# Block 0's x in half rows, W_in in two later parts, block 1's diagonal products in four slots

## The chip, the core and the metric

One kernel, launched once on one NeuronCore of a Trainium2 chip. The metric is device time in microseconds (us), the median of nine runs. TensorE is called PE here, VectorE DVE, ScalarE ACT, GpSimd POOL and SyncE SP, as the profile names them.

## What is computed

The reference is a causal depthwise convolution with seven softmaxed taps for each of eight heads, followed by a two-layer network with an exact GELU:

```
w   = softmax(weight, axis=-1)                       # [8 heads, 7 taps]
xp  = x with 6 zero rows ahead of each sequence      # x: [8, 4096, 192] float32
a[b,s,h,g] = sum_k w[h,k] * xp[b, s+k, h, g]         # 24 channels a head
h   = a.reshape(32768, 192) @ w_in                   # w_in: [192, 2048]
out = (0.5*h*(1+erf(h/sqrt(2)))) @ w_out             # w_out: [2048, 192], float32 out
```

## The kernel before, in words

The 32768 tokens are two halves of 16384, which lie on partitions 0 to 63 and 64 to 127. Each half is cut into 35 blocks: six of 256 tokens (`WS`), then 29 of 512. The 192 channels stand on 64 partitions as three planes (`p`, `NP = 3`), channel 3i+p in plane p. All engine programs are written out by hand; semaphores are the only order between them.

A block goes through these steps. SP loads x in four quarters (`load`, L329). DVE transposes 32x32 tiles into `xT` (`trans`, L526), one instruction a plane. From block 2 on, DVE makes the convolution with seven multiply-adds a plane (`conv`, L552 and L559) and writes `xc` in bf16. PE multiplies `xc` with W_in (`mm1`, L760) in slices into one of two PSUM buffers `hp`; ACT applies the GELU to each slice (L681) and writes `gT`; PE multiplies `gT` of the block before with W_out (`mm2`, L791, `mm2_t` from block 6 on, L824). A slice of `mm1` may start only when the GELU two slices back is done (`S_GELU`). The results leave through `osb`.

Blocks 0 and 1 (`PC`) are different, because DVE would be too slow for a start: their convolution is made on PE (`pconv`, L711), as products of 64x64 diagonal matrices `dg`, one for each tap, with a bf16 copy `xTb` of `xT`. Their four accumulations (`kinds`: plane 0, plane 1, and two halves of plane 2) are called kd 0 to 3; `conv_out` (L191 on ACT, L193 on DVE) copies them from PSUM to `xc`. Block 0's fourteen products for kd 0 and 1 and for kd 2 and 3 come ahead of everything; block 1's stand behind slices 4 and 5 of block 0's `mm1` (the dictionary `behind`, L729).

The start, engine by engine, in program order:

- **SP**: the taps `wsb` (L872), two quarters of block 0's x; then a wait on the first part of W_in (`S_WIN[0]`, L874); block 1's x, W_out in four parts (L878), block 2's and block 3's x. ACT issues the other two quarters of block 0's x. In block 0 a partition holds eight consecutive tokens, and one run of 1440 numbers (5760 bytes) is read for it, both channel halves with it, of which 96 numbers a token are used.
- **POOL**: W_in's first part (256 of 1024 columns a half, L384, two DMAs that cast to bf16), the identity mask (L393), the second part (256 columns) and the third (512); then the halo columns, block 1's bf16 casts (L213, on `xT` of block 1), and the bf16 casts of W_out (L457), which the first `mm2` waits for.
- **DVE**: memsets, the softmax of the taps (L467 to L485), `dg` (L491), block 0's three transposes, two `conv_out` pieces, copies of W_in's parts to the other half's partitions (`dup`, L502; slices 4 to 7 of block 0's `mm1` need them, `S_DUPE`), block 1's transposes, the last `dup`, block 1's six `conv_out` pieces, and then block 2.
- **ACT**: the exponentials, block 0's three bf16 casts (L630), four `conv_out` pieces, then GELUs.
- **PE**: sixteen products of zeros (L695), block 0's diagonal products, then slices.

Of the kernel before, what the change touches and what calls it, by code (L numbers as in the profile page):

```python
# [11 lines left out]
def bass_lightweight_conv__then__act_gelu_exact_kernel(  # L12
# [7 lines left out]
    B, SEQ, D = x.shape  # L20
    H, KS = weight.shape
    D2, F = moe_w_in.shape
# [6 lines left out]
    TB = 512  # L29
# [19 lines left out]
    HX = 8  # L49
# [53 lines left out]
    def sem(name):  # L103
        return es.enter_context(nc.semaphore(name))

    def ap(t, off, pat):
        return bass.AP(t, off, pat)

    with es:
# [23 lines left out]
        ob = pst("ob", [128, 2048])  # L133

        S_WSB = sem("S_WSB")
        S_WIN = [sem("S_WIN%d" % i) for i in range(3)]
        S_WOUT = [sem("S_WOUT%d" % i) for i in range(4)]
        S_WOG = sem("S_WOG")
        S_XIN = [sem("S_XIN%d" % i) for i in range(NX)]
# [6 lines left out]
        S_DG = sem("S_DG")  # L146
        S_HOT = sem("S_HOT")
        S_CAST = [sem("S_CAST%d" % i) for i in range(len(PC))]
        S_PC = sem("S_PC")
        S_PCE = sem("S_PCE")  # L150
        S_PCA = sem("S_PCA")
# [52 lines left out]
        NCV = NP * KS  # L204
        FQ = F // 8
        FH = F // 2
        FP = [0, FQ, 2 * FQ, FH]

        WG = [0, 4, 2, 6]

# [105 lines left out]
        def load(e, n, qs=(0, 2, 1, 3), sm=None):  # L316
            mb = WS[n] // 32
            if n >= NX:
                e.wait_ge(S_TR, NP * (n - NX + 1))
            for q in qs:  # L320
                off = ((q // 2) * HALF + OFF[n]) * D + DQ * (q % 2)
                if n == 0:

                    dst = [[TB // 32 * DQ, 32], [1, mb * D - DQ]]
                    src = [[mb * D, 32], [1, mb * D - DQ]]
                else:
                    dst = [[TB // 32 * DQ, 32], [DQ, mb], [1, DQ]]
# [52 lines left out]
        @block.gpsimd  # L380
        def _(g):
            def win_in(c0, c1, sm):
                for hf in range(2):
                    g.dma_start(  # L384
                        ap(win, 64 * hf * NP * F + c0, [[NP * F, 64], [F, NP], [1, c1 - c0]]),
                        ap(wint, hf * FH + c0, [[NP * F, 64], [F, NP], [1, c1 - c0]]),
                    ).then_inc(sm, 16)

            win_in(FP[0], FP[1], S_WIN[0])
            g.wait_ge(S_MSET, 1)  # L390
            for hf in range(2):
                m = idb[64 * hf : 64 * hf + 64, :]
                g.affine_select(  # L393
                    out=m,
                    in_=m,
                    compare_op=ALU.is_equal,
                    fill=0.0,
                    base=0,
                    pattern=[[-1, 64]],
                    channel_multiplier=1,  # L400
                ).then_inc(S_IDN)
            for i in range(1, 3):
                win_in(FP[i], FP[i + 1], S_WIN[i])

            def halo(n):
                if n == 0:

                    t = xTb[0]
                    g.memset(
                        ap(t, 0, [[NP * XB, 128], [XB, NP], [32, HB]]), 0.0  # L410
                    ).then_inc(S_HALO)
                    for p in range(NP):
                        g.wait_ge(S_TR, p + 1)
                        g.tensor_copy(
                            ap(t, p * XB + 1, [[NP * XB, 128], [32, HB], [1, 31]]),
                            ap(
                                xT[0],
                                p * XW + HX + WS[0] - HL,
                                [[NP * XW, 128], [32, HB], [1, 31]],
                            ),  # L420
                        ).then_inc(S_HALO)
# [25 lines left out]
                g.tensor_copy(dst, src).then_inc(S_HALO)  # L447

            g.wait_ge(S_IDN, 2)
            halo(0)  # L450
            halo(1)
            for p in range(NP):
                cast(g, 1, p)
            for i in range(4):
                g.wait_ge(S_WOUT[i], 16)
                o = 2 * WG[i] * C
                g.tensor_copy(wout[:, o : o + 4 * C], woutf[:, o : o + 4 * C]).then_inc(S_WOG)  # L457
            for n in range(2, NB):
                halo(n)

        @block.vector
        def _(v):
# [34 lines left out]

            def dup(s):

                v.wait_ge(S_WIN[s], 32)  # L500
                for hf in range(2):
                    v.tensor_copy(  # L502
                        ap(
                            win,
                            64 * (1 - hf) * NP * F + FH + FP[s],
                            [[NP * F, 64], [F, NP], [1, FP[s + 1] - FP[s]]],
                        ),
                        ap(
                            win,
                            64 * hf * NP * F + FP[s],  # L510
                            [[NP * F, 64], [F, NP], [1, FP[s + 1] - FP[s]]],
                        ),
                    ).then_inc(S_DUPE)

            def trans(n, p):
                w = WS[n]
                if p == 0:
                    if xin_at(n) > 0:
                        v.wait_ge(S_XIN[n % NX], xin_at(n))
                    if n >= 2 and n - 2 in PC:  # L520
                        wait_pc(v, n - 2, NP - 1)
                    elif n >= 2:
                        v.wait_ge(S_CV, cvd(n - 2))
                    if n >= 1:
                        v.wait_ge(S_HALO, HC[n])
                v.transpose(  # L526
                    ap(xT[n % 2], p * XW + HX, [[NP * XW, 128], [1, w]]),
                    ap(
                        xin[n % NX],
                        p,  # L530
                        [[TB // 32 * DQ, 128], [D if n == 0 else DQ, w // 32], [NP, 32]],
                    ),
                ).then_inc(S_TR)

# [44 lines left out]

            for p in range(NP):  # L580
                trans(0, p)
            conv_out(v, 0, 1)
            conv_out(v, 0, 4)
            dup(0)
            dup(1)
            for p in range(NP):
                trans(1, p)
            dup(2)
            for j in range(len(PIECES)):
                conv_out(v, 1, j)  # L590

# [18 lines left out]
        def _(a):  # L610
# [14 lines left out]
                out=hot[:, 1:2], in_=nc.const_aps.tensor(0.0, (1, 1), F32), func=AF.Gelu  # L625
            ).then_inc(S_HOT)
            a.wait_ge(S_PRO, 9)
            for p in range(NP):
                a.wait_ge(S_TR, p + 1)  # L629
                a.activation(  # L630
                    out=ap(xTb[0], p * XB + HL, [[NP * XB, 128], [1, WS[0]]]),
                    in_=ap(xT[0], p * XW + HX, [[NP * XW, 128], [1, WS[0]]]),
                    func=AF.Copy,
                ).then_inc(S_CAST[0])
# [56 lines left out]
        @block.tensor  # L691
        def _(t):
            t.wait_ge(S_WARM, 1)
            for i in range(16):
                t.matmul(hp[1][:, 0:512], warm[:, 0:128], warm[:, :])  # L695

            def pconv(n, kd, k):

                p, ex, c0, w = kinds(n)[kd]
                if k == KS - 1:  # L700
                    t.wait_ge(S_CAST[PC[n]], p + 1)
                    if n == 0:
                        t.wait_ge(S_DG, 1)
                if k == KS - 2:
# [21 lines left out]
            for kd in order:  # L726
                pconv(*seq[kd].pop(0))

            behind = {  # L729
                (0, 4): [(1, kd, k) for k in taps for kd in (0, 1)],  # L730
                (0, 5): [(1, kd, k) for k in taps for kd in (2, 3)],
            }

            def mm1(n, i):
# [4 lines left out]
                if i == 0:  # L739
                    if n in PC:  # L740
                        wait_pc(t, n, NP - 2)
                    else:
                        t.wait_ge(S_CV, cvd(n))
                if n == 0 and i < 3:
                    t.wait_ge(S_WIN[i], 32)
                if n == 0 and 4 <= i < 7:
                    t.wait_ge(S_DUPE, 2 * (i - 4) + 2)
                for cc in range(c):
                    for p in range(NP):
# [170 lines left out]
```

## Time and profile before

| | |
|---|---|
| median of nine runs | 684.06 us (683.55 to 684.52) |
| the profiled execution | 684.13 us, its span 682.4 us |
| PE busy | 675.5 us, 99% of the span |
| DVE, ACT, POOL busy | 560.9, 536.8, 38.8 us |
| first diagonal product / first slice of `mm1` / first GELU | 7.04 / 8.92 / 10.12 us |
| block 2's first transpose / first slice of block 2's `mm1` | 20.39 / 29.92 us |

All times inside the execution count from the start of the span; 1.7 us of the run's time lie outside it. A line such as `5.96 0.53 DVE xT L526` gives start, length, engine, tile and line of the kernel. "Idle before" is how long the engine stood still, with what released it.

### The profile page before, as it was taken

The page shows a single profiled execution, that of the slowest core. Times are in us where ns is not written, and L with a number is a line of the kernel's source. Part 1 is how long each engine was busy: PE and PEld are TensorE (multiplying, and loading weights), DVE is VectorE, ACT ScalarE, POOL GpSimd, SP SyncE. Part 2 cuts the span into 40 slices and gives each one's busy share as a digit, 9 for nine tenths or more (in the row PEclk, how much of TensorE's full clock was granted, in tenths as well). Part 3 has the DMA queues.
Part 4 walks back from the last instruction along what each step waited for, and adds up shares of the span by engine and source line. Part 5 has one row for each costly group of instructions (what it writes and reads, how often), then busy time and mean ns, then how long its engine had stood idle before and what let it go on. Part 6 is the DMA issues. An engine that isn't in the chain of part 4 may idle for free.

```text
span 682.4 us, 27317 instructions
## 1 busy us (share of the span) xinstructions
PE 675.5 (99%) x12576; PEld 410.2 (60%) x12576; DVE 560.9 (82%) x904; ACT 536.8 (79%) x550; POOL 38.8 (6%) x57
## 2 busy tenths in 40 slices
PE   8999999999999999999999999999999999999998
PEld 4899755555555555555555555555555555555556
DVE  6899979888889888898888898888898888988611
ACT  6799988877777877777877788777778777778772
POOL 5025100000000000000000000000000000000000
PEclk9999999999999999999999999999999999999999
DMA  9345322234342244332244422334322444310123
GB/s 227 72 110 129 84 60 66 45 81 95 96 93 52 46 96 94 95 73 52 67 94 95 94 65 47 81 94 96 93 51 47 95 94 96 79 45 21 48 49 94
DMA packets 132994, 54.79 MB, mean 80 GB/s; under 512 B 126480, under 2 KB 132752, under 8 KB 132880
## 3 DMA queue, kind: packets, MB, share of 16 engines
q1 hardware_dynamic: 130960, 51.50, 32.2%
q8 instruction: 98, 1.61, 1.0%
q0 software_dynamic: 1248, 0.79, 0.9%
q10 hardware_dynamic: 672, 0.76, 0.4%
q14 instruction: 16, 0.13, 0.1%
HBM read 28.66 MB, written 25.17 MB: 79 GB/s over the span
## 4 chain that ended last, share of the span: by engine, by line
PE 96%; ACT 2%; DMA 1%; issue 1%; DVE 0%; SPq 0%; ACTq 0%
PE hp L760 47%; PE ob L824 43%; PE ob L791 5%; ACT gT L681 2%; DMA xin<-in_x_dram 1%; PE ob L711 0%; ACT xc L191 0%; ACT osb L269 0%; DVE osb L311 0%; DVE xT L526 0%; ACT xTb L630 0%; SPq L872 0%; DVE osb L280 0%; SPq L329 0%; ACTq L629 0%
## 5 line engine op out<-in xcount | busy, mean ns | idle before, releaser
L681 ACT ACTIVATE gT<-hp 128x1024 bf16<-128x1024 f32 x512 | 522.8, 1023 | 130.0 <-PE hp L760 126.7
L760 PE MATMUL hp<-xc,win 64*64 64x512 bf16 (+2 forms) x6048 | 419.2, 366 | 2.2 <-issue 0.8
L824 PE MATMUL ob<-gT,wout 64*64 64x512 bf16 x5376 | 366.3, 376 | 0.0
L559 DVE SCALAR_TENSOR_TENSOR acc<-xT,wcol,acc 128x512 f32<-128x512 f32 (+1 forms) x495 | 314.5, 702 | 0.0
L760 PEld LDWEIGHTS hp<-xc,win 64*64 64x64 bf16 (+1 forms) x6048 | 189.9, 106 | 135.4 <-ACT gT L681 2.5
L824 PEld LDWEIGHTS ob<-gT,wout 64*64 64x64 bf16 x5376 | 172.1, 118 | 123.0
L311 DVE STREAM_TRANSPOSE osb<-ob 128x512 f32<-128x512 f32 x84 | 74.3, 887 | 101.0 <-PE ob L824 101.0
L526 DVE STREAM_TRANSPOSE xT<-xin 128x512 f32<-128x512 f32 (+1 forms) x105 | 78.6, 798 | 4.5 <-DMA xin<-in_x_dram 4.5
L559 DVE SCALAR_TENSOR_TENSOR xc<-xT,wcol,acc 128x512 bf16<-128x512 f32 (+1 forms) x99 | 65.2, 715 | 0.0
L447 POOL COPY xT<-xT 128x18 f32<-128x18 f32 x30 | 27.9, 928 | 505.0 <-DVE xT L526 482.6
L791 PE MATMUL ob<-wout,gT 64*128 64x192 bf16 x1024 | 52.9, 243 | 0.3
L791 PEld LDWEIGHTS ob<-wout,gT 64*128 64x128 bf16 x1024 | 44.9, 94 | 5.2 <-PE ob L791 0.6
L552 DVE TENSOR_SCALAR acc<-xT,wcol 128x512 f32<-128x512 f32 (+1 forms) x90 | 37.6, 474 | 1.1
L282 ACT ACTIVATE osb<-ob 128x192 f32<-128x192 f32 x4 | 1.3, 330 | 9.5 <-PE ob L791 9.5
L280 DVE COPY osb<-ob 128x192 f32<-128x192 f32 x4 | 1.4, 358 | 8.4 <-PE ob L791 8.4
L695 PE MATMUL hp<-warm 128*128 128x512 bf16 x16 | 5.5, 517 | 1.3 <-DVE warm L463 1.3
L269 ACT ACTIVATE osb<-ob 128x384 f32<-128x384 f32 x12 | 5.8, 486 | 0.0
L654 ACT ACTIVATE acc<-xT,wcol 128x256 f32<-128x256 f32 (+1 forms) x9 | 5.2, 575 | 0.0
L695 PEld LDWEIGHTS hp<-warm 128*128 128x128 bf16 x16 | 1.9, 126 | 4.3 <-issue 2.5
L384 POOL DMA_DIRECT2D win<-in_moe_w_in_dram x6 | 3.9, 658 | 0.8 <-POOLq L905 0.8
L193 DVE CAST xc<-ob 64x256 bf16<-64x256 f32 (+3 forms) x8 | 2.8, 357 | 1.3 <-PE ob L711 1.1
L502 DVE COPY win<-win 64x768 bf16<-64x768 bf16 (+1 forms) x6 | 3.6, 607 | 0.2
(31 smaller groups left out, 22.1 us busy)
## 6 DMA issues: line engine op xcount, KB each, us to landing
out_dram<-osb SPq DMA_DIRECT2D x122, 192.0 KB, 3.1
xin<-in_x_dram SPq DMA_DIRECT2D x116, 192.0 KB, 4.1
xin<-in_x_dram SPq DMA_DIRECT2D x20, 96.0 KB, 3.7
woutf<-in_moe_w_out_dram SPq DMA_DIRECT2D x4, 384.0 KB, 5.9
win<-in_moe_w_in_dram POOLq DMA_DIRECT2D x4, 96.0 KB, 4.2
win<-in_moe_w_in_dram POOLq DMA_DIRECT2D x2, 192.0 KB, 5.2
out_dram<-osb SPq DMA_DIRECT2D x8, 48.0 KB, 1.9
out_dram<-osb ACTq DMA_DIRECT2D x4, 96.0 KB, 1.9
```

Of the source, the lines that this page charges most:

```text
L269: e.activation(out=dst, in_=src, func=AF.Copy).then_inc(S_EVA)
L311: v.transpose(ap(osb[m % 2], j, [[8 * C, 128], [C // 2, TB // 32], [NP, 32]]), bank(ring(m, j)),).then_inc(S_EV)
L447: g.tensor_copy(dst, src).then_inc(S_HALO)
L526: v.transpose(ap(xT[n % 2], p * XW + HX, [[NP * XW, 128], [1, w]]), ap(xin[n % NX], p, [[TB // 32 * DQ, 128], [D if n == 0 else DQ, w // 3 ...
L552: ins = v.tensor_scalar(a, src, wk, None, ALU.mult)
L559: ins = v.scalar_tensor_tensor(dst, src, wk, a, op0=ALU.mult, op1=ALU.add)
L654: a.activation(out=acc[n % 2][:, p * TB : p * TB + w], in_=ap(xT[n % 2], p * XW + HX, [[NP * XW, 128], [1, w]]), func=AF.Copy, scale=wcol[ ...
L681: a.activation(out=ap(gT[n % 2], i * c * 2 * w, dst), in_=ap(hp[u % 2], 0, src), func=AF.Gelu,).then_inc(S_GELU)
L695: t.matmul(hp[1][:, 0:512], warm[:, 0:128], warm[:, :])
L760: ins = t.matmul(hp[u % 2][fo : fo + fw, o : o + w], ap(win, f1, [[NP * F, 64], [2, fw]]), xc[n % 2][r, p * TB : p * TB + w], start=(p == ...
L791: ins = t.matmul(bank(bb[sub], w=C), gT[m % 2][r, c0 : c0 + 128], wout[r, CH[sub][i] * C : (CH[sub][i] + 1) * C], start=(ph == 0 and i == ...
L824: ins = t.matmul(bank(ring(m, j), slice(64 * h, 64 * h + 64), w), ap(wout, 64 * hf * NF * C + CH[h][i] * C + j, [[NF * C, 64], [NP, 64]],) ...
```

## The change

Block 0's x is read in half rows: 96 numbers (384 bytes) a token, eight runs a partition, so that the four loads move 96 KB each instead of 180 KB. W_in comes in two parts of 512 columns a half instead of three, and POOL issues them all behind the mask and behind a wait for the first result of the softmax, the taps' maximum (`S_PRO` at 1). So `S_WIN[0]`, on which SP waits ahead of block 1's x, now stands for half of W_in. The copies `dup` are four of 256 columns instead of two of 256 and one of 512; the last two stay behind block 1's transposes. Block 0's third bf16 cast goes from ACT to DVE, behind the transposes. Twelve products of zeros instead of sixteen. Block 1's diagonal products stand behind slices 4 to 7 instead of 4 and 5: sixteen and twelve for kd 0 and 1, then sixteen and twelve for kd 2 and 3.

```diff
-        FP = [0, FQ, 2 * FQ, FH]
+        FP = [0, FH // 2, FH]
@@ load
                 if n == 0:
-                    dst = [[TB // 32 * DQ, 32], [1, mb * D - DQ]]
-                    src = [[mb * D, 32], [1, mb * D - DQ]]
+                    src = [[mb * D, 32], [D, mb], [1, DQ]]
@@ POOL
-            win_in(FP[0], FP[1], S_WIN[0])
             g.wait_ge(S_MSET, 1)
...
-            for i in range(1, 3):
+            g.wait_ge(S_PRO, 1)
+            for i in range(2):
                 win_in(FP[i], FP[i + 1], S_WIN[i])
@@ DVE: dup(s) waits for S_WIN[s // 2] and copies FQ columns
             for p in range(NP):
                 trans(0, p)
+            v.wait_ge(S_TR, NP)
+            v.tensor_copy(
+                ap(xTb[0], (NP - 1) * XB + HL, [[NP * XB, 128], [1, WS[0]]]),
+                ap(xT[0], (NP - 1) * XW + HX, [[NP * XW, 128], [1, WS[0]]]),
+            ).then_inc(S_CASTV)
             conv_out(v, 0, 1)
             conv_out(v, 0, 4)
             dup(0)
...
             dup(2)
+            dup(3)
@@ ACT
-            for p in range(NP):
+            for p in range(NP - 1):
                 a.wait_ge(S_TR, p + 1)
@@ PE
-            for i in range(16):
+            for i in range(12):
                 t.matmul(hp[1][:, 0:512], warm[:, 0:128], warm[:, :])
...
             behind = {
-                (0, 4): [(1, kd, k) for k in taps for kd in (0, 1)],
-                (0, 5): [(1, kd, k) for k in taps for kd in (2, 3)],
+                (0, 4): [(1, kd, k) for k in taps[:4] for kd in (0, 1)],
+                (0, 5): [(1, kd, k) for k in taps[4:] for kd in (0, 1)],
+                (0, 6): [(1, kd, k) for k in taps[:4] for kd in (2, 3)],
+                (0, 7): [(1, kd, k) for k in taps[4:] for kd in (2, 3)],
             }
@@ mm1
-                if n == 0 and i < 3:
-                    t.wait_ge(S_WIN[i], 32)
-                if n == 0 and 4 <= i < 7:
+                if n == 0 and i in (0, 2):
+                    t.wait_ge(S_WIN[i // 2], 32)
+                if n == 0 and i >= 4:
                     t.wait_ge(S_DUPE, 2 * (i - 4) + 2)
```

More of the change, by code (lines that the diff above doesn't have):

```diff
@@ L135, in bass_lightweight_conv__then__act_gelu_exact_kernel @@
         S_WSB = sem("S_WSB")
-        S_WIN = [sem("S_WIN%d" % i) for i in range(3)]
+        S_WIN = [sem("S_WIN%d" % i) for i in range(2)]
         S_WOUT = [sem("S_WOUT%d" % i) for i in range(4)]
@@ L148, in bass_lightweight_conv__then__act_gelu_exact_kernel @@
         S_CAST = [sem("S_CAST%d" % i) for i in range(len(PC))]
+        S_CASTV = sem("S_CASTV")
         S_PC = sem("S_PC")
@@ L321, in load @@
                 off = ((q // 2) * HALF + OFF[n]) * D + DQ * (q % 2)
+                dst = [[TB // 32 * DQ, 32], [DQ, mb], [1, DQ]]
                 if n == 0:
-                    dst = [[TB // 32 * DQ, 32], [1, mb * D - DQ]]
-                    src = [[mb * D, 32], [1, mb * D - DQ]]
+                    src = [[mb * D, 32], [D, mb], [1, DQ]]
                 else:
-                    dst = [[TB // 32 * DQ, 32], [DQ, mb], [1, DQ]]
                     src = [[D, 32], [32 * D, mb], [1, DQ]]
@@ L498, in dup @@
             def dup(s):
-                v.wait_ge(S_WIN[s], 32)
+                v.wait_ge(S_WIN[s // 2], 32)
                 for hf in range(2):
@@ L504, in dup @@
                             win,
-                            64 * (1 - hf) * NP * F + FH + FP[s],
-                            [[NP * F, 64], [F, NP], [1, FP[s + 1] - FP[s]]],
-                        ),
[L508 to L512, printed above, removed]
+                            64 * (1 - hf) * NP * F + FH + FQ * s,
+                            [[NP * F, 64], [F, NP], [1, FQ]],
+                        ),
+                        ap(win, 64 * hf * NP * F + FQ * s, [[NP * F, 64], [F, NP], [1, FQ]]),
                     ).then_inc(S_DUPE)
@@ L530, in trans @@
                         p,
-                        [[TB // 32 * DQ, 128], [D if n == 0 else DQ, w // 32], [NP, 32]],
+                        [[TB // 32 * DQ, 128], [DQ, w // 32], [NP, 32]],
                     ),
@@ L700, in pconv @@
                 if k == KS - 1:
-                    t.wait_ge(S_CAST[PC[n]], p + 1)
+                    if n == 0 and p == NP - 1:
+                        t.wait_ge(S_CASTV, 1)
+                    else:
+                        t.wait_ge(S_CAST[PC[n]], p + 1)
                     if n == 0:
```

## The prediction

> **What bounds the kernel now.** The page first: PE is busy for 99% of the span, and nothing after the start is touched by the change, so it acts through the moment at which PE's unbroken work begins. I therefore read the chain of waits over the first 32 us:
>
> ```profile
> 1.64 4.30 DMA xin<-in_x_dram
> 5.93 0.02 issue
> 5.96 0.53 DVE xT L526
> ...
> 7.04 0.97 PE ob L711 x19
> ...
> 17.31 0.77 issue
> 18.08 0.52 PE hp L760 x6
> ```
>
> Block 0's x sets the start; later there is a hole (17.31) in which PE waits for nothing that is shown. Then the timeline of the same stretch, for what stands around these steps:
>
> ```profile
> 4.62 0.62 DVE L491 TENSOR_TENSOR dg<-idb,wcol 128x448 bf16<-128x448 bf16 x1
> ...
> 5.96 1.34 DVE L526 STREAM_TRANSPOSE xT<-xin 128x256 f32<-128x256 f32 x3 [0.72 <-DMA xin<-in_x_dram]
> ...
> 12.51 1.36 DVE L526 STREAM_TRANSPOSE xT<-xin 128x256 f32<-128x256 f32 x3 [1.63 <-DMA xin<-in_x_dram]
> ...
> 20.39 1.34 DVE L526 STREAM_TRANSPOSE xT<-xin 128x256 f32<-128x256 f32 x3 [2.17 <-DMA xin<-in_x_dram]
> ...
> 28.50 1.28 DVE L559 SCALAR_TENSOR_TENSOR xc<-xT,wcol,acc 128x256 bf16<-128x256 f32 x3
> ...
> 29.89 0.14 PEld L760 LDWEIGHTS hp<-xc,win 64*128 64x128 bf16 x4 [0.23 <-issue]
> 29.92 0.29 PE L760 MATMUL hp<-xc,win 64*128 64x256 bf16 x2
> ```
>
> DVE stands still three times for x: 0.72 us ahead of block 0, 1.63 ahead of block 1, 2.17 ahead of block 2. From 20.39 it never stops, its last piece of block 2's `xc` ends at 29.78, and PE starts on it at 29.92, where its own work ends too (29.89). So two chains meet there, PE's own and DVE's from block 2's x, and **the gain is the smaller of their shifts**. Behind it nothing gives it back: block 3 meets the same way (40.33 and 40.47), later blocks have 2.0 to 3.4 us to spare, and from 88 us on PE repeats 20.72 us a block.
>
> Last the stretches (span; PE, PEld, DVE, ACT, POOL; granted clock; DMA share; GB/s), and the queues from 15 to 17 us:
>
> ```profile
> 7.00:8.00 1.00, 0.95 (x32) 0.91 (x36) 0.30 (x1) 0.75 (x2) 0.80 (x3) 1.00 0.90 107
> 8.00:10.00 2.00, 1.66 (x50) 1.20 (x41) 1.52 (x4) 1.30 (x4) 0.00 (x0) 1.00 1.18 224
> 10.00:12.00 2.00, 1.53 (x26) 0.91 (x22) 0.84 (x2) 1.88 (x2) 0.00 (x0) 1.00 1.11 266
> 12.00:15.00 3.00, 2.71 (x58) 1.88 (x58) 2.43 (x5) 2.97 (x4) 1.86 (x4) 1.00 1.05 365
> ```
> ```profile
> q1 hardware_dynamic: 1094, 0.51, 117.5%
> q8 instruction: 1, 0.02, 3.9%
> ```
>
> The DMA engines are full from 2 to 18 us. The one q8 packet is 16 KB of instructions, under way from 15.57 to 16.82 behind W_out; PE resumes at 18.08, after its hole.
>
> **Block 0's x.** Old: 128 packets of 5760 B at 357 ns over 16 engines, 2.86 us. New: 1024 packets of 384 B; such packets took 22 ns each in the first 20 us, so 1.41 us. For the landing the nearest row is block 5's x: four such loads, issued from 33.64 to 35.54, landed by 37.42, 2.3 us behind the start of the last issue. Here the last starts at about 1.75, so x lands at 4.1; the far bound is the slowest load of the start, 8.0 us, too late by far, but that one queued behind W_out. W_in leaves the front of the queue. What is late next is `dg`: DVE works until 5.24, so its transposes start at 5.20 (it starts 0.04 before the end of the one before) instead of 5.96: **-0.76 us**, with 1.1 us of cover. The Trainium skill, DMA: Bandwidth & Descriptors, section Specifications, speaks against this: below 512 B a packet is read, changed and written, short of full rate. Here 384 B in 22 ns are 17.5 GB/s an engine and 5760 B in 357 ns are 16.1, so the row shows no such loss; were the packets half as fast, an estimate from that page's warning, x would take 2.8 us and land at 5.5, which leaves about 0.45 of the 0.76.
>
> **Cast and zeros.** The third cast (0.42 on ACT, 7.33 to 7.75) goes to DVE, which stood still for 1.09 us ahead of its first `conv_out`: hidden, at most 0.43 (the 64x256 cast from PSUM), gain 0 to 0.05, taken as 0. Twelve products of zeros end at about 5.87 (the twelfth starts at 5.49, each takes 0.38), before the diagonal products at 6.28; sixteen would end at 6.73 and cost 0.45. The clock rose at 5.03, after 3.8 us of such products, and both counts outlast that.
>
> **W_in.** The maximum is done at 2.31, so POOL's four issues (0.62 to 0.78 each) run from 2.4 to 5.0, where the last of before ended at 5.83. First packet: before, the third part's came 1.3 us after its issue, so about 4.4 here; the bound is the 2.3 us of the first part, 5.45. At the quick rate of before (200 packets of 1024 B a us, 8.0 to 8.7) half of W_in takes 1.9 us, at the slow one (about 110 from 7 to 8) 3.5. So `S_WIN[0]` comes at 6.5, bounds 6.3 and 8.9; I take 6.5 to 7.5, the quick row being the longer one. PE needs it at 8.13 (8.89 less 0.76): free. SP queues block 1's x, W_out and block 2's x behind this wait, before at 6.73; now 6.5 to 7.5. W_in ends at 8.4 to 9.4 instead of 10.4 (stragglers aside).
>
> **x of blocks 1 and 2.** Their packets stand behind W_in, so they move with its end: by 1.0 to 2.0, less the 0.3 to 0.7 of block 1's x that had already flowed beside it; I take 0.9, bounds 0 and 1.6. Block 1's x then lands at 11.6 instead of 12.49, enough for PE's new clock (it may be 0.76 earlier). Block 2's lands at 19.5 instead of 20.36.
>
> **Four slots and the hole.** Each detour to the diagonal products costs about 0.2 us ahead and behind; by the rows of 13.72 to 14.86 and 15.42 to 16.14 I get 0.69, 0.58, 0.45 and 0.40 us instead of 1.03 and 0.62: 0.47 us more PE time. PE then goes: slice 4 at 12.41, slice 5 at 13.77 (before 14.86), slice 6 at 15.01 (16.14), slice 7 at 16.13 (16.81, its second half at 18.08), the last diagonal product until 17.26. The instruction fetch was asked for at about 9.9 and came after W_out's third load. It now has less before it: ready near 16.9 or sooner, and the same count of instructions is reached at about 17.0, so no hole; were it back as late as 18.08, it would cost some 1.0 here. But DVE now gets kd 2 and 3 last: three pieces at 0.32 from 17.29 end at 18.22, as before (DVE then bound by the old `dup`, until 15.89). Block 1's first slice waits for that, ends at 18.87 and its GELU starts at 18.91 instead of 19.54: **0.63 kept of 0.76**; the next at 19.92 instead of 20.57. PE's shift is 0.65.
>
> **Sum.** PE's chain 0.65, DVE's from block 2's x 0.9 (its other input, 18.22, is no limit): 0.65. From the profiled 684.13, which stands 0.07 above the median, 683.5.
>
> **The rivals.** *DVE's chain does not move*: if block 2's x still lands at 20.36 (the engine that fetches instructions ran 2 us behind the others), PE waits at 29.9 and gains 0 to 0.1: 684.0. For it: one engine's shares landed from 19.4 to 20.36, all others by 18.5. Against: there are 0.34 MB less in front. *W_in too late, slower*: if POOL's loads start at 5.45 and flow at the slow 110 to 122, half lands at 8.6 to 8.9 and the whole ends at 11.8 to 12.4, 1.4 to 2.0 later than now; block 2's x, and with it DVE and PE at 29.9, come by as much later: 685.5 to 686.1. It decides once W_in's end passes 10.4. For it: the slow stretch from 7 to 8, in which nothing else flowed. *More than the sum, faster*: a cold product of zeros takes 427 ns and a warm one 216. In an execution whose clock rises late, sixteen end at 1.26 + 16 x 0.427 = 8.09 and hold PE 1.05 us; twelve end at 6.38. Then the gain is 0.65 + 1.05: 682.4. For it: the nine runs differ by 0.97 us; against: the profiled one, with an early rise, is no faster than the median. The same skill's page TensorE: Matmul & The Clock Gate, Part 1, has a free-running window of 3.4 us, which would allow it; no run here shows it.
>
> **How the numbers follow.** 0.2% is 1.37 us, about what a measurement of this kernel can tell from no change. Forecast 0.47 (0.43 within, 0.04 faster by the faster bounds of both chains); DVE's chain still 0.13, all within; W_in late 0.22 (0.18 slower, 0.04 a mild form within); late clock 0.18, faster. So 0.22, 0.60, 0.18. The forecast alone spans 683.2 to 684.1. The range runs from 682.3 to 685.8: it takes in the third rival and the nearer half of the second.
>
> **What would show it.** Right: first transpose at 5.2, first diagonal product at 6.3, no DMA wait ahead of it; `S_WIN[0]`'s wait on SP over by 7.5; no hole near 17; GELU of block 1 at 18.9; block 2's transposes before 19.7 and its first slice at 29.3. Wrong: PE waiting on W_in at 8.1, block 1's x after 11.7, or block 2's transposes after 20.4.

## The result, and the profile after

The changed kernel takes **686.50 us** (nine runs, 685.52 to 687.32) against 683.94 us of the kernel before (29 runs beside it): a ratio of 1.0038 with a 95% interval of 1.0029 to 1.0046, 2.56 us slower. A tenth run, which this median leaves out, took 684.45, only 0.5 us more than before; with it the median is 686.49. The forecast was 683.5. The profiled execution took 687.02 us, its span 685.3; before it was 684.13 and 682.4, so the two profiles differ by 2.89.

The chain of waits of the kernel after, its first 33 us (start, length, what; `SPq` is an issue on SP's queue):

```profile
2.63 0.80 POOL win L383
3.43 6.01 DMA win<-in_moe_w_in_dram
9.45 0.02 issue
9.46 0.35 SPq L328
...
11.33 0.45 SPq L885
...
12.85 3.20 SPq L885
16.05 0.04 issue
16.09 0.47 SPq L328
...
17.60 5.71 DMA xin<-in_x_dram
23.31 0.02 issue
23.33 1.35 DVE xT L522 x3
...
32.72 0.14 issue
32.86 0.83 PE hp L767 x12
```

Before, the chain went through block 0's x and then PE. Now it goes from POOL's first W_in load to SP, which stands at `S_WIN[0]` until 9.46, through eight issues of SP in a row (block 1's x, then W_out), the last of which takes 3.20 us, to block 2's x, which has landed at 23.31, DVE's convolution of block 2, and PE's first slice of block 2 at 32.86. That slice is 2.94 us later than before (29.92), which is the whole difference of the two executions: the time less the start of this slice is 684.13 - 29.92 = 654.21 before and 687.02 - 32.86 = 654.16 after.

The timeline of the kernel after, the same stretch:

```profile
5.17 1.33 DVE L522 STREAM_TRANSPOSE xT<-xin 128x256 f32<-128x256 f32 x3
...
9.58 1.49 PE L767 MATMUL hp<-xc,win 64*128 64x256 bf16 x24 [1.64 <-DMA win<-in_moe_w_in_dram]
...
13.32 1.35 DVE L522 STREAM_TRANSPOSE xT<-xin 128x256 f32<-128x256 f32 x3 [2.08 <-DMA xin<-in_x_dram]
...
23.05 0.83 PE L798 MATMUL ob<-wout,gT 64*128 64x192 bf16 x16 [1.64 <-POOL wout L457]
23.33 1.34 DVE L522 STREAM_TRANSPOSE xT<-xin 128x256 f32<-128x256 f32 x3 [3.58 <-DMA xin<-in_x_dram]
```

Block 0's transposes start at 5.17 without any wait (5.96 before), and the gain ends there: PE stands 1.64 us for W_in ahead of 9.58, where before it began at 8.92. Block 2's transposes wait 3.58 us, and PE waits once more, for W_out's last cast, ahead of 23.05.

The stretches (us; busy time of PE, PEld, DVE, ACT, POOL; granted clock; DMA share; GB/s), the queues between 4 and 8 us, and the instruction queue between 12 and 17 us, all of the kernel after:

```profile
7.00:8.00 1.00, 0.94 (x42) 0.75 (x34) 0.41 (x2) 0.74 (x2) 0.18 (x2) 1.00 0.84 96
8.00:10.00 2.00, 0.42 (x8) 0.45 (x10) 0.77 (x4) 0.57 (x3) 0.00 (x0) 1.00 1.05 168
10.00:12.00 2.00, 1.52 (x29) 1.26 (x27) 1.18 (x3) 1.55 (x2) 0.00 (x0) 1.00 0.64 152
12.00:15.00 3.00, 2.56 (x42) 1.45 (x40) 1.65 (x4) 2.95 (x4) 1.06 (x3) 1.00 0.98 252
```
```profile
q0 software_dynamic: 442, 0.42, 89.2%
q1 hardware_dynamic: 205, 0.07, 8.0%
```
```profile
q8 instruction: 1, 0.02, 3.8%
```

From 10 to 12 us the DMA engines are busy for 64%, where they were over-full before (1.11): SP's loads, issued only from 9.46 on, left a gap. And W_in's half consists of 384 packets, but from 4 to 8 us 442 packets had moved in POOL's queue, 414 of W_in and 28 that only count up a semaphore (`q0` is POOL's queue, `q1` SP's); still `S_WIN[0]` came only at 9.45. Each of the half's two loads is split over 16 engines, and these 32 shares end far apart. The fetch of 16 KB of instructions takes 3.8% of 16 engines x 5 us = 3.0 us, 12.59 to 15.67 (1.25 us before, 15.57 to 16.82); SP's issue of 3.20 us is the one that was under way meanwhile. From this fetch on, one of 16 shares comes late in each of W_out's four loads: at 17.59, 18.61, 20.21 and 22.12, where the other fifteen are in by 14.82, 16.45, 17.43 and 19.02. The last of these is what PE's wait ahead of 23.05 goes back to. Block 2's x has such stragglers too, its last five shares of 64 from 22.32 to 23.31 and the others by 21.34, as it had before (the last four from 19.42 to 20.36, the others by 18.50). The trace does not name the engine of a share.

### The profile page after: what moved, and what is told of

Read it like the earlier page. It is cut to its first block, busy times and chain, and to the rows that moved or that the text cites. A ratio compares the mean times of both kernels' runs of the same rounds, so it can differ in the third digit from the quotient of the medians.

```text
span 685.3 us, 27310 instructions
## 1 busy us (share of the span) xinstructions
PE 675.4 (99%) x12572; PEld 410.1 (60%) x12572; DVE 561.0 (82%) x907; ACT 536.5 (78%) x549; POOL 37.6 (5%) x55
## 4 chain that ended last, share of the span: by engine, by line
PE 93%; DMA 2%; DVE 1%; ACT 1%; SPq 1%; issue 1%; POOL 0%
PE hp L767 46%; PE ob L831 42%; PE ob L798 5%; ACT gT L683 1%; DMA win<-in_moe_w_in_dram 1%; DMA xin<-in_x_dram 1%; DVE acc L555 1%; SPq L885 1%; SPq L328 0%; DVE xT L522 0%; DMA wsb<-in_weight_dram 0%; ACT osb L270 0%; DVE osb L312 0%; POOL win L383 0%; DVE acc L548 0%
## 5 line engine op out<-in xcount | busy, mean ns | idle before, releaser
L502 DVE COPY win<-win 64x768 bf16<-64x768 bf16 x8 | 3.4, 420 | 1.4 <-DMA win<-in_moe_w_in_dram 1.2
L716 PE MATMUL ob<-xTb,dg 64*64 64x128 bf16 (+1 forms) x112 | 3.9, 248 | 0.3 <-ACT xTb L632 0.2
```

## The experiments

In every kernel run the time of the profiled execution less the start of block 2's first slice lies between 654.13 and 654.23 us, and that slice starts either 9.53 us behind block 2's first transpose (DVE's chain) or later (PE's chain); in e8_late_place PE's own chain ends there as well. So a run is read from two columns. "SP" is the start of block 1's x, the first thing behind SP's wait.

| kernel | median / before beside it | ratio, 95% | profiled | SP | transposes of block 2 | slice of block 2 | set by |
|---|---|---|---|---|---|---|---|
| before | 684.06 | | 684.13 | 6.73 | 20.39 | 29.92 | DVE |
| after | 686.50 / 683.94 | 1.0029 to 1.0046 | 687.02 | 9.46 | 23.33 | 32.86 | DVE |
| e1_sp_on_dg | 685.11 / 683.73 | 1.0012 to 1.0030 | 685.05 | 5.28 | 20.14 | 30.88 | PE |
| e2_three_parts | 685.60 / 683.73 | 1.0020 to 1.0037 | 684.80 | 6.43 | 19.80 | 30.62 | PE |
| e3_first_early | 687.53 / 683.73 | 1.0040 to 1.0067 | 687.53 | 8.33 | 22.57 | 33.39 | PE |
| e4_half_rows | 683.99 / 683.73 | 0.9995 to 1.0012 | 683.77 | 6.38 | 19.78 | 29.64 | PE |
| e5_slots | 684.33 / 683.95 | 0.9997 to 1.0014 | 684.55 | 6.68 | 19.59 | 30.41 | PE |
| e6_two_parts | 686.06 / 683.95 | 1.0024 to 1.0049 | 684.56 | 8.76 | 20.86 | 30.39 | DVE |
| e7_sp_two_slots | 684.89 / 683.95 | 1.0007 to 1.0025 | 684.74 | 5.27 | 20.71 | 30.60 | PE |
| e8_late_place | 685.14 / 683.76 | 1.0009 to 1.0027 | 685.64 | 6.99 | 21.94 | 31.47 | both |
| e9_sp_late | 686.74 / 683.76 | 1.0027 to 1.0054 | 686.33 | 10.17 | 22.62 | 32.15 | DVE |
| e10_half_512 | 685.35 / 683.96 | 1.0008 to 1.0027 | 684.05 | 7.52 | 20.36 | 29.89 | DVE |
| e11_sp_first_xc | 685.03 / 683.86 | 1.0003 to 1.0021 | 685.15 | 8.54 | 21.39 | 30.92 | DVE |
| e12_sp_first_xc_after | 685.29 / 683.86 | 1.0011 to 1.0029 | 684.77 | 7.86 | 20.52 | 30.64 | PE |
| e13_half_512_look | one run, 685.39 | | 685.39 | 9.21 | 21.67 | 31.20 | DVE |
| c1_order | 686.09 / 683.95 | 1.0020 to 1.0049 | 684.27 | 6.74 | 17.66 | 30.08 | PE |
| c2_sp_on_dg | 684.06 / 683.76 | 0.9995 to 1.0013 | 684.34 | 5.32 | 20.05 | 30.19 | PE |
| c3_behind_mask | 684.32 / 683.76 | 0.9995 to 1.0013 | 684.47 | 6.10 | 19.76 | 30.30 | PE |
| c4_order | 685.43 / 683.96 | 1.0016 to 1.0033 | 685.44 | 6.58 | 18.02 | 31.26 | PE |

### What SP's wait costs

**e1_sp_on_dg: the kernel after, SP's wait taken off W_in.**

```diff
-            sp.wait_ge(S_WIN[0], 32)
+            sp.wait_ge(S_DG, 1)
```

> The changed kernel, but SP waits for dg (about 5.2 us) instead of for half of W_in (9.45 us) ahead of block 1's x. Theory 1, the wait: half of W_in behind SP's wait holds block 1's x, W_out and block 2's x back by 2.7 us, and block 2's x sets DVE's chain. Then block 2's first transpose comes at 20.4 or sooner instead of 23.3, and the time is 684.0 or less, as before the change. Theory 2, the flow: W_in is slow in itself (about 120 packets of 1024 B a us) and everything shares the same engines, so block 1's x only slows W_in: first slice after 9.6, block 2's first transpose after 22, 685.5 or more.

Block 2's transposes went back from 23.33 to 20.14, and half of the loss with them: 685.11, which is neither expectation. The other half stays. Now PE sets the end, and two lines of its timeline show where it stood:

```profile
9.60 1.49 PE L767 MATMUL hp<-xc,win 64*128 64x256 bf16 x24 [1.34 <-DMA win<-in_moe_w_in_dram]
12.08 1.49 PE L767 MATMUL hp<-xc,win 64*128 64x256 bf16 x24 [0.99 <-DMA win<-in_moe_w_in_dram]
```

So the change has two costs that lie side by side: W_in comes late to PE, and it comes late to SP. (In PE's part lie the four slots as well, see below.)

**e9_sp_late: the kernel before, with only SP's wait made longer** (until ACT's fourth copy of block 0's convolution).

```diff
-            sp.wait_ge(S_WIN[0], 32)
+            sp.wait_ge(S_PCA, 4)
```

> The kernel before, except that SP waits ahead of block 1's x until ACT's last copy of block 0's convolution (about 9.42 us), which is where half of W_in let it go in the changed kernel (9.45). W_in, block 0's x and everything else stay. Theory 1, the wait: the whole shift of block 2's x is here, first transposes of block 2 at 22.5 to 23.3, 685.9 to 686.7. Theory P, PE's late W_in is half of it: block 2's x lands before 22 and the time is 684.5 to 685.5.

With W_in, slots and x as before, the moment at which SP goes on is alone worth as much as the whole change: 686.74 with SP at 10.17 (9.46 in the kernel after). In its chain the wait stands as x of block 1, W_out and block 2's x, one behind the other:

```profile
10.17 0.33 SPq L329
...
12.02 1.58 SPq L878
...
16.78 5.81 DMA xin<-in_x_dram
```

**e12_sp_first_xc_after and e11_sp_first_xc: SP waits for ACT's first copy**, in the kernel after (SP at 7.86) and in the kernel before (8.54).

```diff
-            sp.wait_ge(S_WIN[0], 32)
+            sp.wait_ge(S_PCA, 1)
```

> The kernel after, with the same edit: SP goes on at about 7.7 instead of 9.46; W_in as in the kernel after. Theory 'W_in for PE, its wait for SP': PE still waits for the half until about 9.5 and for the second part, so 685.0 to 685.4, as where SP goes on at 5.3 (685.1), with block 2's first transpose before 21.6. Rival 'any wait on SP': 685.7 to 686.2, half way between 685.1 and 686.5, with block 2's transposes near 22.

> The kernel before, with one edit: SP waits for ACT's first copy of block 0's convolution instead of for the first part of W_in, so that block 1's x is issued from about 8.5 instead of 6.7, at a time that no share of W_in sets. Theory 'shares': what makes the waits for half of W_in long is the one share that lands last, at 7.5 in some executions and past 9 in others; a wait that ends at 8.5 every time then costs little and the runs lie close together: 683.9 to 684.6, within a us of each other. Rival 'any wait on SP': what counts is how much later SP goes on; between 6.7 (nothing lost) and 10.2 (2.7 to 3.0 lost) a wait until 8.5 should cost about half, 685.0 to 685.6.

The first came out for its theory: 685.29 is the floor that PE's wait for W_in sets (685.11 with SP at 5.28). The second came out for the rival: ten of its eleven runs lie between 684.84 and 685.40, close together as the theory had it, but 1.2 us up. With W_in unchanged, then, the medians stand 0.3 (SP at 5.32, an interval that holds no difference), 0 (6.73), 1.2 (8.54) and 3.0 (10.17) us above before: past about 7.5 (where an execution of e10_half_512, below, still loses nothing) SP's lateness costs nearly its full length. The profiled execution of e6_two_parts below, SP at 8.76 and 684.56, lies under this line.

**e10_half_512 and e13_half_512_look: the kernel before, SP waits for two quarters**, that is for as many bytes of W_in as in the kernel after, in packets of 512 B.

```diff
             sp.wait_ge(S_WIN[0], 32)
+            sp.wait_ge(S_WIN[1], 32)
```

> The kernel before, except that SP waits for the second quarter of W_in as well, so for half of it, as with two parts, but in packets of 512 B and issued as before. Theory half (waiting for half is what costs, however it is cut): the time goes to 685.5 or more, as with two parts (686.1). Theory packets (the half is late because 1024 B packets start slowly): it lands at 7.5, SP goes on 0.8 later, block 2's x at 20.4 to 21.2, 683.8 to 684.6.

The eleven runs fell in two groups, five from 683.54 to 684.91 and six from 685.35 to 686.29, and the profile had one of the lower, in which nothing was lost; the median, 685.35, lies between the two expectations. A second profile of the same kernel:

> The kernel before in which SP waits for the second quarter of W_in as well, a second look by profile at a kernel whose times lay in two groups, 683.5 to 684.9 and 685.4 to 686.3. Theory 'shares': an execution of the upper group shows the last share of the second quarter past 8.8 where the others are in by 7.4, and block 2's transposes after 21.3. Rival: the upper group shows the second quarter in by 7.6, and loses its time elsewhere. An execution of the lower group tells nothing new.

This time the profile has a longer one. The chains, first the lower, then the longer one:

```profile
3.97 3.46 DMA win<-in_moe_w_in_dram
...
7.52 0.33 SPq L329
...
20.36 1.35 DVE xT L526 x3
```
```profile
3.97 5.16 DMA win<-in_moe_w_in_dram
...
9.21 0.33 SPq L329
...
12.06 2.25 SPq L879
...
16.37 5.28 DMA xin<-in_x_dram
```

Thirty of the 32 shares of the second quarter were in by 7.40, the last two came at 8.05 and 9.12. In the lower execution all were in by 7.43. So a wait for half of W_in is a wait for its slowest share, which differs by 1.7 us from run to run, and SP hands that on: 685.39 - 684.05 = 1.34 us. The other traces agree: in the ten executions that issue quarters at the old place, the second quarter's last share comes between 7.43 and 9.12, the first quarter's, for which SP waits before, always between 6.36 and 6.80. PE is spared, because it needs this quarter only at 9.92.

**c2_sp_on_dg: the kernel before, SP waits for nothing of W_in.**

```diff
-            sp.wait_ge(S_WIN[0], 32)
+            sp.wait_ge(S_DG, 1)
```

> The kernel before with SP waiting for dg (5.2 us) instead of the first quarter of W_in (6.7 us). Block 2's x lands 0.5 to 1.5 sooner, but PE's chain ends at the same 29.9 and now W_in's last part has block 1's x beside it: theory 1 gives 683.5 to 684.0 (no gain, as PE's chain is not moved), theory P 684.2 to 684.8 (W_in later, PE's chain late).

No gain. Block 1's x flows beside W_in, whose end moves from 10.77 to 11.83, and PE's third slice waits for it until 11.96 (11.21). The old wait, for a quarter, was near the best place between the two costs.

### What W_in's place and parts cost

**e8_late_place: the kernel before, its three parts all issued behind mask and maximum.**

```diff
-            win_in(FP[0], FP[1], S_WIN[0])
             g.wait_ge(S_MSET, 1)
...
-            for i in range(1, 3):
+            g.wait_ge(S_PRO, 1)
+            for i in range(3):
```

> The kernel before with one part of the change alone: all three parts of W_in behind the mask and the taps' maximum. Theory 1, the wait on SP explains everything: the first quarter lands at 7.0 to 7.5 instead of 6.7, so at most 0.7 later: 683.9 to 684.5. Theory P, the late place costs PE's chain by itself: W_in's last part lands 1 us later, slice 2 and block 1's products with it, 684.7 to 685.2.

685.14, +1.4, as theory P had it. The first quarter is little later (6.97 instead of 6.71), the last part 1.9 us (12.69 instead of 10.77): the third slice starts at 12.82 and block 1's x lands at 14.21.

**e2_three_parts: the kernel after, W_in in three parts at the same late place.**

```diff
-        FP = [0, FH // 2, FH]
+        FP = [0, FQ, 2 * FQ, FH]
...
-            for i in range(2):
+            for i in range(3):
```

(`dup` and `mm1` wait for the three parts in turn.)

> The changed kernel with W_in in three parts again (256, 256, 512 columns), all at the new place behind the taps' maximum. Theory 1, the wait: the first part stands for a quarter, lands at 6.2 to 7.0, SP goes on then, block 2's x lands by 20.4, and the start of the transposes at 5.2 remains: 683.3 to 684.0. Theory 2, the flow: where W_in is issued is what costs; the first quarter lands after 7.5, 685 or more. The packets of 512 B show also whether only those of 1024 B are slow: then the first quarter flows at 350 a us or more, otherwise at about 240.

685.60, +1.9 where the kernel after has +2.6; neither expectation, and the profiled execution is the fastest of the eleven. The quarters landed at 6.41 and 8.36, where the half of the kernel after took until 9.45; SP went on at 6.43 and PE started at 8.92. But six issues keep POOL until 6.53, the halo comes late (PE stands for 0.56 us ahead of 7.20), and the third part lands at 11.86. Packets of 512 B flowed at about 270 a us here, not at the 350 or more of the old place.

**e6_two_parts: the kernel before, W_in in two parts at the old, early place.**

```diff
-        FP = [0, FQ, 2 * FQ, FH]
+        FP = [0, FH // 2, FH]
...
-            for i in range(1, 3):
+            for i in range(1, 2):
```

(With the copies in quarters and the waits that belong to it.)

> The kernel before with W_in in two parts and the copies in quarters, both parts issued where the three were (the first ahead of the mask); block 0's x in whole rows. Theory 1, the wait on SP: half of W_in behind it lands at 8.3 or later instead of 6.7, SP's queue moves by 1.6 or more, and block 2's x too: 684.8 to 686. Theory L, the late place alone matters: issued early, two parts cost nothing: 683.5 to 684.1. If packets of 1024 B are slow from the start, the part's packets show some longer than 140 ns, of which the 512 B ones had one in 768.

686.06, with the widest spread of all (684.44 to 689.83); the profiled execution is near its lower end, so its trace shows only part of the loss. Even there the half landed at 8.75, 2.0 us behind the first quarter, for which SP waits in the kernel before (6.71). So a half is late for SP although it is issued as early as ever. Whether it is later than two quarters of the same bytes (7.43 to 9.12 in ten executions) one trace does not tell. What its longest runs have beyond that no trace shows.

**e3_first_early: the kernel after, the first half issued ahead of the mask.**

```diff
+            win_in(FP[0], FP[1], S_WIN[0])
             g.wait_ge(S_MSET, 1)
...
             g.wait_ge(S_PRO, 1)
-            for i in range(2):
-                win_in(FP[i], FP[i + 1], S_WIN[i])
+            win_in(FP[1], FP[2], S_WIN[1])
```

> The changed kernel with the first of the two parts (half of W_in) issued at POOL's old place, ahead of the mask; the second part stays behind the maximum. Theory 1, the wait: the half starts 1.3 us sooner, lands at about 8.0 instead of 9.45, and the time falls by as much as SP goes on sooner: 684.8 to 685.3. Theory 2, the flow: the packets of 1024 B are slow until 8 us wherever they are issued; the half still lands after 9 and block 0's x is pushed to 5.5 as well: 686 or more.

687.53, the slowest of all. The half landed at 8.31, but now block 0's x, in packets of 384 B, came at 8.73 instead of 4.92. From 2 to 5 us the two queues that carry x moved 412 packets here and 1088 in the kernel after; first this kernel, then that:

```profile
q0 software_dynamic: 158, 0.16, 46.6%
q10 hardware_dynamic: 275, 0.10, 12.3%
q1 hardware_dynamic: 137, 0.05, 9.9%
```
```profile
q10 hardware_dynamic: 544, 0.20, 28.7%
q1 hardware_dynamic: 544, 0.20, 27.9%
q0 software_dynamic: 77, 0.08, 23.6%
```

PE then stood still for 3.64 us ahead of 9.84, and its granted clock fell (columns as above):

```profile
6.00:9.00 3.00, 0.20 (x1) 0.00 (x0) 0.24 (x1) 0.00 (x0) 0.00 (x0) 1.00 1.19 203
9.00:12.50 3.50, 2.66 (x56) 2.51 (x56) 1.81 (x5) 1.63 (x5) 1.30 (x4) 0.51 0.82 208
```

### The other parts alone, and tries at a faster one

**e4_half_rows: the kernel before, block 0's x in half rows.**

```diff
-                    src = [[mb * D, 32], [1, mb * D - DQ]]
+                    src = [[mb * D, 32], [D, mb], [1, DQ]]
```

> The kernel before with one part of the change alone: block 0's x in half rows. The prediction's first step: x lands before 5.2 and the transposes start at 5.2 instead of 5.96. Theory 1 adds that the first quarter of W_in lands 0.8 to 1.2 us sooner too, so SP's queue and block 2's x move with it and the gain arrives: 683.2 to 683.5. Theory 3, the hole: PE's stop at 17 to 18 us for its instructions takes the gain back: 683.9 to 684.2, with block 2's transposes still near 20.4.

No difference. Beside W_in at its old place x in half rows landed at 6.53, later than whole rows did (5.94). Block 2's x gained a little (transposes at 19.78), block 1's did not (12.63, before 12.51).

**e5_slots: the kernel before, four slots. e7_sp_two_slots: e1_sp_on_dg with the old two slots.** The edit is the dictionary `behind` of the diff alone, there forwards, here backwards.

> The kernel before with one part of the change alone: block 1's diagonal products in four slots instead of two. By the prediction's own terms they take 0.47 us more of PE, and the last ones come after slice 7, so that DVE's last three copies (1.0 us) stand between them and block 1's first slice. Theory S, the slots cost: block 1's first GELU moves from 19.54 to 20.0 or later, PE's chain is 0.4 to 1.0 late at block 2's first slice, 684.2 to 684.8. Theory F, the fetch hides it: PE's stop for instructions near 17 to 18 us falls behind the same count of instructions in either order and the slots fill it, so nothing changes: 683.5 to 684.0.

> The changed kernel with SP waiting for dg (as the earlier run, 685.1) and block 1's diagonal products in the two old slots. Theory S, the slots cost: their 0.5 us and the copies behind them go, so 684.2 to 684.7. Theory W, PE's chain is late only because W_in and block 1's x land late (first slice 9.6, block 1's x 13.6): 684.9 to 685.3, the slots being worth less than 0.2.

The slots cost 0.4 in the kernel before, where the interval (0.9997 to 1.0014) still holds no difference, and about as much where the change is otherwise kept: e1_sp_on_dg lost 1.38, e7_sp_two_slots 0.94, in intervals that overlap. So a price of 0.4 is likely, but neither pair shows it clear of noise.

**c1_order and c4_order: the kernel before, block 2's x ahead of W_out's last two parts**, `dup(2)` ahead of block 1's transposes; c1_order also waits for block 1's x there.

```diff
+                if i == 2:
+                    sp.wait_ge(S_XIN[1], 64)
+                    load(sp, 2)
...
-            load(sp, 2)
```

> The kernel before with another order, from what the runs showed: SP waits for block 1's x behind W_out's second part, then loads block 2's x and W_out's last two parts; DVE makes its last copy of W_in ahead of block 1's transposes, where it stood still for 1.63 us. If queue order is what sets both chains, block 2's transposes start at 17.5 to 18.5 instead of 20.4, the instruction fetch has less before it and PE's hole at 17 is shorter by 0.5 or more: 683.0 to 683.4. If PE's chain stays where it is (the hole remains), the time stays within 0.2 of 683.7. If W_out comes too late for the first product with it (after 20.3), 684.5 or more.

> The kernel before with block 2's x ahead of W_out's last two parts (no added wait on SP) and DVE's last copy of W_in ahead of block 1's transposes. DVE's chain then starts block 2 at 18.0 to 19.0 instead of 20.4. If PE's chain stands by itself, with its hole for instructions near 17 to 18, the time stays at 683.6 to 684.0; if the hole and the copies were what held PE, 683.0 to 683.4; if W_out's last parts come too late, 684.3 or more.

Block 2's x came 2.4 to 2.7 us earlier, as wanted, and both kernels are slower. PE now waits for W_out; c4_order's timeline:

```profile
18.02 1.34 DVE L526 STREAM_TRANSPOSE xT<-xin 128x256 f32<-128x256 f32 x3 [0.38 <-DMA xin<-in_x_dram]
...
21.01 0.83 POOL L457 CAST wout<-woutf 128x768 bf16<-128x768 f32 x1 [0.97 <-DMA woutf<-in_moe_w_out_dram]
21.89 0.83 PE L791 MATMUL ob<-wout,gT 64*128 64x192 bf16 x16 [1.42 <-POOL wout L457]
```

**c3_behind_mask: what seemed sound of the change**: half rows, cast on DVE, twelve products of zeros, quarter copies; W_in in three parts right behind the mask without the wait for the maximum; two slots.

```diff
-            g.wait_ge(S_PRO, 1)
-            for i in range(2):
+            for i in range(3):
```

> A mixture meant to be faster: the changed kernel's half rows, twelve products of zeros, cast on DVE and copies in quarters, with W_in in three parts right behind the mask (no wait for the maximum) and the diagonal products in the two old slots. If what cost was half of W_in behind SP's wait, its late place and the slots, what remains is the early start: transposes at 5.2 to 5.4, first slice 8.2 to 8.9, 683.0 to 683.6. If W_in beside the small packets of block 0's x holds these back, as in the run with half rows alone, the transposes start at 5.8 or later: 683.8 to 684.5.

No gain: x came at 5.73 and the first slice started at 8.70 (8.92), but W_in's end moved to 11.47 and the third slice to 11.60 (11.21). No version beat the kernel before.

## Why the prediction was wrong

**The frame held.** The gain was to be the smaller of two chains' shifts, meeting at block 2's first slice, with nothing given back behind it. The shift of that slice, +2.94, is the difference of the executions, and the table's kernels all obey it. The sign of both shifts was wrong: DVE's +2.94 instead of -0.9, and PE's about +2.6 instead of -0.65 (its profile has PE stand 0.3 us for DVE ahead of that slice). With SP's wait taken off W_in PE's shift is still +0.96 (e1_sp_on_dg).

**"W_in" is the step that failed.** `S_WIN[0]` was to come at 6.5 to 7.5, at worst 8.9; it came at 9.45. The first packet came at 4.15 (4.4 foretold), so the flow was mis-sized, in two ways. First the rate: 200 packets a us had been taken, from a row of the second half of W_in; from 4 to 8 us 442 packets moved, 110 a us, which was the *slow* row. At that rate the half's 384 packets end at about 7.6, past the 7.5 that had been taken. Then the end: the first half's shares are not done together. 28 of the 32 were in at 8.18 and the last at 9.45, and the engines that were ahead had already gone on to the second part. The prediction knew a share that lands 2 us behind the others from block 2's x and did not ask the same of W_in. At the late place the larger part is the later one: the half came at 9.10 to 9.46 in four executions (the kernel after, e1_sp_on_dg, e7_sp_two_slots, e12_sp_first_xc_after), two quarters at 8.02 and 8.36 (e8_late_place, e2_three_parts). At the early place that is not shown: 8.75 for the half (e6_two_parts), 7.43 to 9.12 for two quarters. Early and steady at both places is a first quarter alone (6.36 to 6.80, and 6.41 and 6.97 at the late place).

**"W_in" again: the queue behind the wait.** The text named what stands on SP behind this wait, and then let it cost nothing as long as W_in's end moved forward. e9_sp_late and e11_sp_first_xc show that it has a price of its own: block 2's x comes later nearly us for us once the DMA engines run dry (64% busy from 10 to 12). Beyond that block 2's x stands 1.67 us later in the kernel after than in e13_half_512_look (23.31 and 21.64, SP at 9.46 and 9.21). The longer issue beside the instruction fetch (3.20 against 2.25) is a likely part of it; no run takes it away, so it is argued and not shown.

**"x of blocks 1 and 2"** followed from W_in's end, 8.4 to 9.4; it was 11.42. Block 1's x landed at 13.30 (11.6 foretold), block 2's at 23.31 (19.5).

**"Block 0's x" was right, on a condition.** Landing 4.92 instead of 4.1, transposes at 5.17 (5.20 foretold), first diagonal product at 6.25 without a wait for a DMA. But e4_half_rows and e3_first_early show that half rows are quick only because W_in was moved out of their way: the 0.76 was bought with W_in's lateness, and PE gave it back at once in 1.64 us of waiting. The skill's warning about packets below 512 B, weighed there, showed little while x had the engines nearly to itself: 22 ns a packet at the median, 17.5 GB/s an engine, and 26 ns, 14.8 GB/s, on average, where the whole rows of before averaged 338 ns, 17.0 GB/s. Beside larger packets x did badly, and for that the Trainium skill, DMA: Bandwidth & Descriptors, section "Queues, rings and completion order", has a rule that was not weighed: an engine serves its queues in turn, packet by packet. By that rule the queue with the smaller packets would move fewer bytes. The queues of e3_first_early agree: from 3.5 to 5 us `q0` moved 117 packets of up to 1024 B (0.12 MB) and `q1` 116 of up to 384 B (0.04 MB).

**"Cast and zeros" was right**: the cast on DVE took 0.29 and held nobody up, and twelve products sufficed.

**"Four slots and the hole" was right in its parts.** The hole near 17 is gone, in e1_sp_on_dg too, where the instruction fetch ended only at 17.38. DVE's last copies stand behind the last diagonal product as foretold. The slots cost about 0.4 (0.47 foretold), which is not clear of noise. The hole's end was no gain, since DVE's copies took its place, and block 1's first GELU came at 20.47 (18.91 foretold) with what stands ahead of it as late: slice 5 at 15.34 (13.77 foretold), the last diagonal product until 18.79 (17.26 foretold).

**The rivals.** "W_in too late, slower" is what happened, with its place and its test: W_in's end at 11.42 is past its 10.4. It was priced at 685.5 to 686.1 and given 0.22, because the kernel's own slow row was read as the exception. Its price went by W_in's end alone, and left out SP's queue, which brought the rest (686.50 against 685.11 in e1_sp_on_dg). "DVE's chain does not move" did not occur: block 2's x came later. "More than the sum, faster" did not either: no run was below 684.45. But its mechanism, which no run had shown when the prediction was written, is in the traces: the granted clock rose between 4.07 and 7.31 us in the sixteen that record the rise. In e9_sp_late, with 7.28, sixteen products of zeros lasted until 7.84 and the first slice started at 9.61 instead of 8.92. In the changed kernel PE waits for W_in until 9.58, and twelve products instead of sixteen can gain nothing ahead of that.

**What stays open.** Why W_in's packets of 1024 B, which the DMA casts, go at 110 a us until 8 us while those of 512 B go at over 300 in the kernel before is not settled: 90 of its 768 packets took over 140 ns (98 is usual), together 25 us of engine time, against one 512 B packet of the kernel before and 15 of e2_three_parts. Nor is it known what the run of 684.45 did otherwise. Nor, last, what the longest runs of e6_two_parts and c1_order (up to 689.83) meet; their traces are of shorter ones.

## What to carry to other kernels

A wait on a loaded buffer is a wait for the slowest share of all its engines; before giving a queue such a wait, list everything that is issued behind it, and give it the smallest part that does its work. Price a transfer by the slowest row of the same packet size and the same time, and price its end by its last share, not by bytes over rate. Where two chains meet, an improvement of one start (here 0.76 us) is worth nothing until both inputs of the next step, here x and W_in, are shown to come in time.

## What the runs showed of the hardware

**SP's issues and instruction fetches.** In every profiled execution an issue on SP that overlaps the first instruction fetch takes 1.1 to 3.2 us, where most take 0.45 (some of 1.0 to 1.4 us stand apart from any fetch). Which load it strikes depends on the order: before, block 3's x (2.71 us, from 15.40), which nobody missed; after, W_out's last part, ahead of block 2's x. Where SP goes on late the fetch mostly comes early: it starts between 12.2 and 13.7 us in all five kernels in which SP goes on at 8.5 or later, and at 15.6 in the kernel before. But it starts at 12.2 with SP at 7.52 too (e10_half_512), and at 17.2 with SP at 8.33 (e3_first_early), so SP's moment alone does not set it. The Trainium skill, Runtime: NRT & Kernel Launch, section "Instruction fetch mechanics", calls the cost of crossing from one 16 KB block of instructions to the next mostly hidden. Here the issue beside the fetch stands 2.75 us too long (3.20 less 0.45) on the chain that sets the end. Whether the fetch holds SP up, which would not be hidden, or both wait for the same engine the runs do not tell.

**A clock that falls.** PE's pause of 3.64 us in e3_first_early was followed by a granted clock of 0.51 from 9.0 to 12.5; the pauses of 1.64 us in the kernel after left it at 1.00. The trace of e3_first_early records the clock's steps: full from 5.69, half from 9.10, full again from 12.52, two stretches of 3.41 us each. The Trainium skill, TensorE: Matmul & The Clock Gate, Part 1, has a free-running window of 3.4 us for this, which agrees.
